# Retention and a Swish layer in one kernel: a fence for each half of the output banks, four up tiles in token halves, two groups of batch 1 a half-up sooner

## The chip, the cores and the metric

The kernel runs on one core of a Trainium2 chip. The core has five engines that run on their own and wait for one another by semaphores: TensorE (PE in the profile; its weight loads are PEld), VectorE (DVE), ScalarE (ACT), GpSimd (POOL) and SyncE (SP), which here issues the DMAs. TensorE multiplies a loaded operand of up to 128 x 128 by a moving one and writes to PSUM, eight banks of 128 partitions. The metric is the device time of one execution in microseconds (us). Before the change the median of 3 runs is 292.82 us (292.6 to 293.25).

## The reference

There are 8 batches, 8 heads, 576 positions and a head size of 64. A retention layer without softmax comes first: scores of q and k, weighted with a decay by distance and cut off above the diagonal, times v. Its output, 4608 tokens of 512 features, goes through two matrix products with a Swish between them.

```python
scores = scale * np.matmul(q, k.transpose(0, 1, 3, 2))
gamma = 1.0 - 2.0 ** (-5.0 - np.arange(H, dtype=np.float32))
Dmat = np.where(rel >= 0, gamma[:, None, None] ** rel[None, :, :], 0.0)
attn = np.matmul(scores * Dmat, v)                 # rel = position of the query less that of the key
x = attn.transpose(0, 2, 1, 3).reshape(B * S, H * D)
h = x @ w_in                                       # 512 -> 2048
out = (h / (1.0 + np.exp(-beta * h))) @ w_out      # 2048 -> 512
```

## The kernel before

**Blocks.** The first 512 positions of each batch are a block of 512 tokens (blocks 0 to 7). The last 64 positions of all eight batches form block 8, the "tails". For each block the retention output is made transposed in `xT` (features on the partitions, in four chunks `ko` of 128), and then come 16 "ups": `up(m, fo)` multiplies a 128-wide tile of `w_in` by the block's `xT`, four matmuls of 512 columns that add up in one PSUM bank, and ACT takes Swish of it into `gT` (L775; from block 3 on every other tile goes by way of `hs`, L772, and DVE, L773). `up(m, fo, c0, cn)` with `cn=2` is a half-up: the same tile for half of the block's tokens, four matmuls of 256 columns. Blocks 0 to 2 then multiply `gT` by `w_out` directly (`down`, L893). From block 3 on the second product is made by seven products of quarter size instead of eight: DVE adds pairs of quarters of `gT` into `sa` (L789), and PE multiplies in the chains U, W and Z (L805).

**Retention.** With the decay folded into q, k and v as gains by position, the work of a batch falls into small matmuls on quarters of TensorE's array: 64 rows by 64 columns each, named by `half(x)` or `row_d(j)`, the first or second 64 partitions. `paired` (L544) writes two lists alternately, so that neighbouring matmuls use different halves of the rows. For batches 2 to 7, `scores` makes the masked score tiles `R`, the states (running sums of k times v over chunks of positions, in `sbd` and `sbq`) are made by `one_state` and added up by `fold`, and `both4` makes the block's output in four PSUM banks `O4[x, y]`, x the parity of the chunk and y the half of the heads:

- `outputs4` (L643): 64 matmuls of `vn` by `R` open and fill the banks, first for y = 0, then for y = 1.
- `fence` (L555): ACT copies 128 x 2 numbers (L556) after the last matmul written so far. Nobody reads the copy; it is there so that the next matmul of another row half on the same bank can wait for it.
- `crosses4` (L661): 56 matmuls of the states by q add the part that comes from earlier chunks. They are 28 pairs, j = 0 and j = 1. j is the row half, and the column half is j for y = 0 and 1 - j for y = 1. Each j first adds to the banks x = j and then to the others. The first cross of j = 0 on x = 1 waits for the fence, the thirteenth pair where nothing else lies between. In batches 3, 5 and 6 sixteen pairs of the next batch's states (`ahead`) stand between the two parts. In both parts y is the innermost loop.

`tail_outputs` (L720) and `tail_crosses` (L735) do the same for the tails with 64 outputs and 64 crosses, and the fence is waited for behind the first 32. All of these matmuls are issued by `mm`, so the profile puts them on L550.

**Batch 1** is done in an older form, by groups (one group is one chunk of 128 positions; 4 to 7 are batch 1's). TensorE turns k around with `t_k` (L414, DVE copies the result, L415), `a_sc` makes scores that DVE masks (L448), `states` and `state_out` make the states, and `second(6)` makes the output of groups 6 and 7 and copies it to `xT` (L499).

**Order.** Engines take their instructions in the order in which the program writes them. `merged` (L913) writes a list of filling work, `fill` (ups, downs and the seven products), one entry after another, and before entry n all steps whose due time is at most n. `u1` is the place of block 1's first half-up. The ten half-ups from `u1` use the first half of block 1's tokens (groups 4 and 5), the ten after them the second half (groups 6 and 7). Their PSUM banks are three of the tag `mm`; scores of batch 1's last groups use the tags `sc` and `O`, two banks each, and `sc` is also where `t_k` puts its result.

Of the kernel before, what the change touches and what calls it, by code (L numbers as in the profile page):

```python
# [19 lines left out]
def kernel(  # L20
# [10 lines left out]
    nc = tc.nc  # L31
# [4 lines left out]
    P = 128  # L36
    HP = H // 2
    KO = d_model // P
    FO = d_ff // P
    MB = 512  # L40
    CB = MB // P
    PC = P // CB
    TL = S - MB
    NT = B // 2
# [5 lines left out]
    SB = 3  # L50
# [115 lines left out]
    for x in range(2):  # L166
        w = slice(x * TL, (x + 1) * TL)
# [15 lines left out]
    w_in_sb = wpool.tile([P, KO, d_ff], BF16, name="w_in_sb")  # L183
# [101 lines left out]
    xts = {}  # L285
# [6 lines left out]
    def F(f, *a):  # L292
        return lambda: f(*a)  # L293
# [4 lines left out]
    batch, pair, live = {}, {}, {}  # L298
# [118 lines left out]
    def q_cols(i, r, p, kind=None):  # L417

        b, c = seq[i]
        cols = slice(c * PC, (c + 1) * PC) if kind is None else slice(c * PC + kind * PC // 2, c * PC + (kind + 1) * PC // 2)  # L420
        return batch[b]["qT"][r, :, p, cols], lambda o: o.rearrange("k (i s) -> k i s", i=CB)
# [112 lines left out]
    def half(x):  # L534
        return slice(x * TL, (x + 1) * TL)

    def row_d(j):
        return slice(j * D, (j + 1) * D)

    def tile_of(c, kind):  # L540

        return c - c % 2 + (c % 2 if kind else 1 - c % 2)

    def paired(one, two):  # L544
        for a, b in zip(one, two, strict=True):
            a()
            b()

    def mm(out, lhsT, rhs, start=False, stop=True, after=None):
        ins = nc.tensor.matmul(out, lhsT, rhs, start=start, stop=stop, skip_group_check=True)  # L550
        if after:
            tc.add_manual_dep(ins.ins, after.pop().ins.name, ordered, reason="row tiles of one bank")
        last[0] = ins

    def fence():  # L555
        f = nc.scalar.copy(fenced[:], lscale[:].to_broadcast([P, 2]))  # L556
        tc.add_manual_dep(f.ins, last[0].ins.name, ordered, reason="row tiles of one bank")
        return [f]
# [13 lines left out]
    def state_banks():  # L572
        return [psum.tile([P, 2, HP, D], F32, name="st", tag=t, bufs=n) for t, n in (("mm", 3), ("st", 1))]
# [64 lines left out]
    def new_O4(lead, shape):  # L638
        live[lead]["O4"] = {(x, y): psum.tile(shape, F32, name="O", tag="sc" if x else "O", bufs=2)
                            for x in range(2) for y in range(2)}  # L640
        return live[lead]["O4"]

    def outputs4(b):  # L643

        i0 = b * CB
        O4, opened = new_O4(i0, [P, 2, CB, 2 * PC]), set()
        R = batch[b]["R"]

        def one(x, y, cc, pp, kind, hh):
            p, c = 2 * y + pp, 2 * cc + x  # L650
            w = cc * PC + kind * PC // 2
            mm(O4[x, y][row_d(hh), pp, :, w:w + PC // 2], live[i0 + tile_of(c, kind)]["vn"][half(x), 2 * p + hh, :],
               R[cc][half(x), hh ^ y, kind, p, :].rearrange("k (i s) -> k i s", i=CB), start=(x, y, hh) not in opened, stop=False)
            opened.add((x, y, hh))

        for y in range(2):
            paired(*[[F(one, x, y, cc, pp, kind, hh ^ x) for cc in range(2) for pp in range(2) for kind in range(2)
                      for hh in range(2)] for x in range(2)])
        batch[b]["O4"] = O4, fence()

    def crosses4(b, later=None):  # L661

        i0 = b * CB
        O4, after = batch[b]["O4"]

        def cross(j, e, y, pp, after):
            p, c, kind = 2 * y + pp, e // 2, e % 2
            w = c // 2 * PC + kind * PC // 2
            mm(O4[c % 2, y][row_d(j ^ y), pp, :, w:w + PC // 2], sbq[e - 1][row_d(j), p, :],
               q_cols(i0 + c, row_d(j), p, kind)[0], after=after)  # L670

        def crosses(j, x, after=None):
            return [F(cross, j, e, y, pp, after) for e in range(1, 2 * CB) if e // 2 % 2 == x for pp in range(2) for y in range(2)]

        ahead, bank = ([], []), None
        if b < B - 1 and b not in (XB, SB + 1):
            bank = state_banks()
            ahead = four_states(b + 1, 0, bank)
        paired(*[crosses(j, j) + ahead[j] + crosses(j, 1 - j, None if j else after) for j in range(2)])
        def out(n, x, y, O):  # L680
            to = xt(b)[:, 2 * y:2 * y + 2].rearrange("k p i (c x s) -> k (p i) c x s", c=2, x=2)[:, :, :, x, :]
            e = nc.scalar.copy if n == 1 or b > XB and n % 2 or later is not None else nc.vector.tensor_copy
            e(to, O[:].rearrange("k p i (c s) -> k (p i) c s", c=2))

        outs = [F(out, n, x, y, O) for n, ((x, y), O) in enumerate(O4.items())]
        if later is not None:
            casts = []
            if bank:
                fold(b + 1, 0, bank, casts=casts, by=nc.scalar.copy)
            later += outs + casts  # L690
            return
        for f in outs:
            f()
        if bank:
            fold(b + 1, 0, bank)
# [24 lines left out]
    def tail_outputs(i0):  # L720

        O4, opened, R = new_O4(i0, [P, 2, NT, TL]), set(), live[i0]["R"]

        def one(x, y, t, pp, hh):
            p = 2 * y + pp
            mm(O4[x, y][row_d(hh), pp, t, :], live[i0 + t]["vn"][half(x), 2 * p + hh, :],
               R[t // 2][half(x), hh ^ y, t % 2 * HP + p, :], start=(x, y, hh) not in opened, stop=False)
            opened.add((x, y, hh))

        for y in range(2):  # L730
            paired(*[[F(one, x, y, t, pp, hh ^ x) for t in range(NT) for pp in range(2) for hh in range(2)]
                     for x in range(2)])
        live[i0]["O4"] = O4, fence()

    def tail_crosses(i0, later):  # L735

        O4, after = live[i0]["O4"]

        def cross(j, x, t, y, pp, after):
            p = 2 * y + pp  # L740
            mm(O4[x, y][row_d(j ^ y), pp, t, :], ends[2 * t + x][row_d(j), p, :], live[i0 + t]["qkT"][row_d(j), 0, p, half(x)],
               after=after)

        for own in range(2):
            paired(*[[F(cross, j, j ^ own, t, y, pp, after if own else None) for t in range(NT) for pp in range(2) for y in range(2)]
                     for j in range(2)])
        def out(x, y, O):
            for r in range(2):
                to = xt(B)[:, 2 * y:2 * y + 2].rearrange("k p (a r) (s l x) -> k (p a) r l x s", r=2, l=2, x=2)[:, :, r, :, x, :]
                nc.scalar.copy(to, O[:].rearrange("k p (a l) (r s) -> k (p a) r l s", l=2, r=2)[:, :, r])  # L750

        later += [F(out, x, y, O) for (x, y), O in O4.items()]
# [4 lines left out]


    gts = {}

    def up(m, fo, c0=0, cn=CB):
        if m not in gts:
            gts[m] = sb.tile([P, FO, CB, P], BF16, name="gT", tag="gT", bufs=1)
        w = slice(c0 * PC, (c0 + cn) * PC)
        ph = psum.tile([P, CB, P], F32, name="ph", tag="mm", bufs=3)
        ph = ph.rearrange("f i s -> f (i s)")[:, :cn * P].rearrange("f (i s) -> f i s", i=CB)
        for ko in range(KO):
            nc.tensor.matmul(ph, w_in_sb[:, ko, fo * P:(fo + 1) * P], xts[m][:, ko, :, w],  # L768
                             start=(ko == 0), stop=(ko == KO - 1))
        if m >= SB and fo % 2:  # L770
            h = scratch[0][:, fo // 2 % 4].rearrange("f (i s) -> f i s", i=CB)
            nc.scalar.activation(h, ph, ACT.Silu, scale=beta_sb[:, fo:fo + 1])  # L772
            nc.vector.tensor_scalar(gts[m][:, fo], h, ratio[:, fo // 2:fo // 2 + 1], None, ALU.mult)  # L773
            return
        nc.scalar.activation(gts[m][:, fo, :, w], ph, ACT.Silu, scale=beta_sb[:, fo:fo + 1])  # L775
# [223 lines left out]
    d0 = len(fill)  # L999
# [9 lines left out]
    u1 = len(fill)  # L1009
# [12 lines left out]
    def second(i):  # L1022
# [3 lines left out]
        if i > CB:  # L1026
# [14 lines left out]
               [(d0 + 12.6, F(t_k, 1, 0, 0)), (d0 + 12.6, F(t_k, 1, 0, 1)), (d0 + 14, F(a_sc, 1, 0, 0)), (d0 + 14, F(a_sc, 1, 0, 1)),  # L1041
                (d0 + 14, F(states, 1, 0)), (d0 + 14, F(state_out, 1, 0)), (d0 + 14, F(state_out, 1, 1)), (d0 + 15.9, F(second, 4))],
               [(d0 + 10, F(pre_k, 1, 1, r)) for r in range(2)] + [(d0 + 12, F(pre_v, 1, 1, r)) for r in range(2)] +
               [(d0 + 15.95, F(t_k, 1, 1, 0)), (u1 + 1, F(t_k, 1, 1, 1)), (u1 + 3, F(a_sc, 1, 1, 0)), (u1 + 3, F(a_sc, 1, 1, 1)),
                (u1 + 3, F(states, 1, 2)), (u1 + 3, F(state_out, 1, 2)), (u1 + 8.5, F(second, 6))]]


    def group1(b, ccs):
# [31 lines left out]
    t = base[2]  # L1080
# [20 lines left out]
    for n in range(SB, B + 1):  # L1101
        t, m = base[n], blocks[n]
        first, second = slice(0, KH // 2), slice(KH // 2, KH)
# [10 lines left out]
    for n in range(1, B):  # L1114
# [3 lines left out]
        b, t = n + 1, base[n]  # L1118
# [61 lines left out]
```

## Time and profile before

| | |
|---|---|
| median of 3 runs | 292.82 us (292.6 to 293.25) |
| profiled execution, its own time | 293.46 us |
| its span in the profile | 291.8 us |
| granted TensorE clock | 1.000 |
| TensorE busy | 280.2 us, 96% |
| VectorE, ScalarE, GpSimd busy | 64%, 58%, 46% |

The profile is one execution, taken by the hardware. Its first part gives each engine's busy time; a list of waits gives who stood idle for whom; a timeline gives, for a stretch of time, the start of a row (us from the span's start), its length, engine, line, operation, output and inputs, shape and count, and in brackets the idle time before it with what ended it. `<-issue` means that nothing in the profile ended that idle time. Ends of matmuls are modelled: a row of n matmuls lasts from the first's start to the last's modelled end, so that neighbouring rows overlap by about 0.2 us. Where the text says "from start to start" it takes the starts alone.

### The profile page before, as it was taken

Reading aid. Unit: us, or ns where it says so; the run is one execution under the profiler, and the core shown is the slowest. Engines: PE = TensorE matmul, PEld = TensorE weight load, DVE = VectorE, ACT = ScalarE, POOL = GpSimd, SP = SyncE. Lnnn points to the kernel's source line nnn. Section 1 sums busy time; section 2 is a strip of 40 time slices with the busy share of each in tenths; the row PEclk is TensorE's granted clock in tenths of the full one; section 3 lists DMA queues with packets and bytes.
Section 4 is the critical chain, followed back from the end, with each engine's and each line's share of the span. In section 5 each row is a group of like instructions: output and inputs, shape, how many; then the busy total and the mean of one; then the engine's idle time right before and its main releaser. Section 6 shows DMA issues by size and latency. Waiting matters only on the chain.

```text
span 291.8 us, 8653 instructions
## 1 busy us (share of the span) xinstructions
PE 280.2 (96%) x3599; PEld 177.4 (61%) x3627; DVE 187.6 (64%) x347; ACT 169.5 (58%) x298; POOL 133.0 (46%) x258
## 2 busy tenths in 40 slices
PE   7899999999999999999999899999999999999995
PEld 5674446764544455548845685578557855784584
DVE  5974545704795296299598794986498545642673
ACT  4377636686968873674157514762476156837730
POOL 6366029924980972678583593434079300000000
PEclk9999999999999999999999999999999999999999
DMA  7999999969999999999999928960678530003004
GB/s 223 309 365 385 380 306 283 189 127 239 186 196 284 222 163 260 283 234 162 255 258 182 246 62 231 175 141 2 205 163 171 81 146 3 0 24 122 0 3 143
DMA packets 120568, 54.05 MB, mean 185 GB/s; under 512 B 93889, under 2 KB 113361, under 8 KB 120529
## 3 DMA queue, kind: packets, MB, share of 16 engines
q1 hardware_dynamic: 120496, 53.49, 76.5%
q8 instruction: 28, 0.46, 0.6%
q14 instruction: 12, 0.09, 0.1%
q10 hardware_dynamic: 32, 0.01, 0.0%
HBM read 36.71 MB, written 9.44 MB: 158 GB/s over the span
## 4 chain that ended last, share of the span: by engine, by line
PE 88%; DVE 5%; DMA 3%; issue 2%; SPq 1%; ACT 0%; POOL 0%; DVEq 0%
PE ph L768 37%; PE po L893 14%; PE U L805 10%; PE Z L805 7%; PE W L805 6%; PE O L550 4%; PE ph L860 4%; DMA kvn<-in_k_dram 3%; PE sc L550 2%; DVE sa L789 2%; PE st L550 2%; DVE sbd L293 1%; PE ph L875 1%; DVE sum L586 1%; PE st L510 1%
## 5 line engine op out<-in xcount | busy, mean ns | idle before, releaser
L768 PE MATMUL ph<-xT,w_in_sb 128*128 128x512 bf16 (+1 forms) x542 | 114.2, 363 | 2.2 <-issue 0.6
L768 PEld LDWEIGHTS <-w_in_sb 128*128 128x128 bf16 x560 | 53.5, 98 | 56.1 <-DVE sum L586 0.9
L775 ACT ACTIVATE gT<-ph,beta_sb 128x512 bf16<-128x512 f32 (+1 forms) x92 | 58.3, 640 | 44.5 <-PE ph L768 43.5
L805 PEld LDWEIGHTS <-sa 128*128 128x128 bf16 x480 | 46.9, 98 | 6.3 <-issue 0.6
L773 DVE TENSOR_SCALAR gT<-hs,ratio 128x512 bf16<-128x512 f32 x48 | 25.8, 539 | 34.4 <-ACT hs L772 33.9
L789 DVE TENSOR_TENSOR sa<-gT 128x1024 bf16<-128x1024 bf16 (+1 forms) x54 | 44.5, 866 | 0.7 <-PE Z L805 0.4
L330 POOL TENSOR_TENSOR qs<-qn,gq 128x256 bf16<-128x256 f32 x48 | 31.9, 696 | 28.1 <-DMA qn<-in_q_dram 20.8
L772 ACT ACTIVATE hs<-ph,beta_sb 128x512 f32<-128x512 f32 x48 | 33.0, 687 | 20.0 <-PE ph L768 19.7
L893 PE MATMUL po<-w_out_sb,gT 128*128 128x512 bf16 x184 | 42.0, 379 | 1.0 <-issue 0.8
L312 POOL TENSOR_TENSOR vn<-kvn,gv 128x256 bf16<-128x256 f32 x48 | 33.3, 714 | 7.6 <-issue 3.2
L367 POOL CAST kn<-kvn 128x128 bf16<-128x128 f32 (+1 forms) x72 | 25.0, 383 | 17.2 <-DMA kvn<-in_k_dram 17.1
L893 PEld LDWEIGHTS <-gT 128*128 128x128 bf16 x192 | 18.1, 98 | 20.9
L805 PE MATMUL U<-b,sa 128*128 128x256 bf16 x192 | 22.9, 273 | 0.4 <-DVE ot L819 0.4
L805 PE MATMUL Z<-b,sa 128*128 128x256 bf16 x192 | 23.1, 273 | 0.0
L293 DVE TENSOR_TENSOR R<-sc,late 128x512 bf16<-128x512 f32 x24 | 15.4, 679 | 11.2 <-issue 10.0
L805 PEld LDWEIGHTS <-gT 128*128 128x128 bf16 x192 | 18.7, 98 | 3.5
L255 DVE TENSOR_TENSOR b<-wt 128x512 bf16<-128x512 f32 x20 | 15.9, 851 | 1.9 <-ACT wt L238 1.8
L448 DVE TENSOR_TENSOR R<-sc,causal 128x512 bf16<-128x512 f32 x16 | 10.2, 682 | 2.2 <-PE sc L550 2.0
L379 POOL CAST kn<-kvn 128x512 bf16<-128x512 f32 x6 | 3.8, 653 | 16.9 <-DMA kvn<-in_k_dram 16.9
L805 PE MATMUL W<-b,gT 128*128 128x256 bf16 x96 | 11.5, 273 | 0.0
L805 PE MATMUL W<-b,sa 128*128 128x256 bf16 x96 | 11.5, 273 | 0.0
L805 PE MATMUL U<-b,gT 128*128 128x256 bf16 x96 | 11.5, 273 | 0.0
(121 smaller groups left out, 316.7 us busy)
## 6 DMA issues: line engine op xcount, KB each, us to landing
qn<-in_q_dram SPq DMA_DIRECT2D x16, 512.0 KB, 5.6
out_dram<-ot SPq DMA_DIRECT2D x32, 256.0 KB, 3.2
wt<-in_moe_w_out_dram SPq DMA_DIRECT2D x8, 512.0 KB, 9.4
kvn<-in_k_dram SPq DMA_DIRECT2D x12, 256.0 KB, 6.6
kvn<-in_v_dram SPq DMA_DIRECT2D x12, 256.0 KB, 5.9
kvn<-in_k_dram SPq DMA_DIRECT2D x24, 128.0 KB, 4.7
kvn<-in_v_dram SPq DMA_DIRECT2D x24, 128.0 KB, 3.8
wt<-in_moe_w_in_dram SPq DMA_DIRECT2D x5, 512.0 KB, 8.3
```

The source lines that it names most:

```text
L293: return lambda: f(*a)
L312: nc.gpsimd.tensor_tensor(vn[:, hs], v[:, hs], g[:, hs], ALU.mult)
L330: nc.gpsimd.tensor_tensor(batch[b]["qs"][:, cs, to], q_tiles[b][:, hs, cs].rearrange("p h i d -> p i h d"), gq[:, cs, hs].unsqueeze(3).to_ ...
L367: nc.gpsimd.tensor_copy(kn[:, c % 2, to], t[:, 0, hs])
L550: ins = nc.tensor.matmul(out, lhsT, rhs, start=start, stop=stop, skip_group_check=True)
L768: nc.tensor.matmul(ph, w_in_sb[:, ko, fo * P:(fo + 1) * P], xts[m][:, ko, :, w], start=(ko == 0), stop=(ko == KO - 1))
L772: nc.scalar.activation(h, ph, ACT.Silu, scale=beta_sb[:, fo:fo + 1])
L773: nc.vector.tensor_scalar(gts[m][:, fo], h, ratio[:, fo // 2:fo // 2 + 1], None, ALU.mult)
L775: nc.scalar.activation(gts[m][:, fo, :, w], ph, ACT.Silu, scale=beta_sb[:, fo:fo + 1])
L789: nc.vector.tensor_tensor(sums_a[0][:, held_in[j], ks], quarter(m, *x, ks), quarter(m, *y, ks), op)
L805: nc.tensor.matmul(chains[c, n][:, 0 if alone else p], a, sevens[k // 2][:, j - 1, k % 2, :], start=j in (3, 4, 1) and k == 0 and (alone o ...
L893: nc.tensor.matmul(po[:, :nn], gT[:, fo, ms, :], w_out_sb[:, fo, n0:n0 + nn], start=(fo == 0), stop=(fo == FO - 1))
```

## The change

It has three parts.

1. `outputs4` and `tail_outputs` make a fence behind the outputs of y = 0 and another behind those of y = 1, and hand on a list of two. In the crosses y becomes the outermost loop in place of the innermost, and the first cross of j = 0 onto the other banks waits for the fence of its own y.
2. In `up`, for block 3 (`SB`) and the tiles 12 to 15, each matmul of 512 columns becomes two of 256, one for each half of the tokens, with the same loaded operand.
3. In batch 1's steps for the last two groups, scores, states and state copies are due at `u1 + 2` instead of `u1 + 3`, and the output of groups 6 and 7 at `u1 + 7.5` instead of `u1 + 8.5`; as entries are whole numbers, each is written one half-up sooner.

```diff
@@ outputs4 (tail_outputs alike)
+        after = []
         for y in range(2):
             paired(*[[F(one, x, y, cc, pp, kind, hh ^ x) for cc in range(2) for pp in range(2) for kind in range(2)
                       for hh in range(2)] for x in range(2)])
-        batch[b]["O4"] = O4, fence()
+            after.append(fence())
+        batch[b]["O4"] = O4, after
@@ crosses4
-        def crosses(j, x, after=None):
-            return [F(cross, j, e, y, pp, after) for e in range(1, 2 * CB) if e // 2 % 2 == x for pp in range(2) for y in range(2)]
+        def crosses(j, x, after=(None, None)):
+            return [F(cross, j, e, y, pp, after[y]) for y in range(2) for e in range(1, 2 * CB) if e // 2 % 2 == x for pp in range(2)]
...
-        paired(*[crosses(j, j) + ahead[j] + crosses(j, 1 - j, None if j else after) for j in range(2)])
+        paired(*[crosses(j, j) + ahead[j] + crosses(j, 1 - j, (None, None) if j else after) for j in range(2)])
@@ tail_crosses
-            paired(*[[F(cross, j, j ^ own, t, y, pp, after if own else None) for t in range(NT) for pp in range(2) for y in range(2)]
-                     for j in range(2)])
+            paired(*[[F(cross, j, j ^ own, t, y, pp, after[y] if own and not j else None) for y in range(2) for t in range(NT)
+                      for pp in range(2)] for j in range(2)])
@@ up
+    halved = (12, 13, 14, 15)
...
+        ns = 2 if m == SB and fo in halved else 1
         for ko in range(KO):
-            nc.tensor.matmul(ph, w_in_sb[:, ko, fo * P:(fo + 1) * P], xts[m][:, ko, :, w],
-                             start=(ko == 0), stop=(ko == KO - 1))
+            for n in range(ns):
+                cs = slice(n * CB // ns, (n + 1) * CB // ns)
+                nc.tensor.matmul(ph[:, cs], w_in_sb[:, ko, fo * P:(fo + 1) * P], xts[m][:, ko, cs, w],
+                                 start=(ko == 0 and n == 0), stop=(ko == KO - 1), skip_group_check=ns > 1)
@@ batch 1's steps
-               [(d0 + 15.95, F(t_k, 1, 1, 0)), (u1 + 1, F(t_k, 1, 1, 1)), (u1 + 3, F(a_sc, 1, 1, 0)), (u1 + 3, F(a_sc, 1, 1, 1)),
-                (u1 + 3, F(states, 1, 2)), (u1 + 3, F(state_out, 1, 2)), (u1 + 8.5, F(second, 6))]]
+               [(d0 + 15.95, F(t_k, 1, 1, 0)), (u1 + 1, F(t_k, 1, 1, 1)), (u1 + 2, F(a_sc, 1, 1, 0)), (u1 + 2, F(a_sc, 1, 1, 1)),
+                (u1 + 2, F(states, 1, 2)), (u1 + 2, F(state_out, 1, 2)), (u1 + 7.5, F(second, 6))]]
```

More of the change, by code (lines that the diff above doesn't have):

```diff
@@ L728, in one @@
             opened.add((x, y, hh))
+        after = []
         for y in range(2):
@@ L732, in tail_outputs @@
                      for x in range(2)])
-        live[i0]["O4"] = O4, fence()
+            after.append(fence())
+        live[i0]["O4"] = O4, after
     def tail_crosses(i0, later):
```

## The prediction

> **What bounds the kernel now.** First the page's head and queue table, then TensorE's (PE's) own waits (us in total, times, longest): is PE the bound, and where does it stand still?
>
> ```profile
> span 291.8 us, 8653 instructions
> PE 280.2 (96%) x3599; PEld 177.4 (61%) x3627; DVE 187.6 (64%) x347; ACT 169.5 (58%) x298; POOL 133.0 (46%) x258
> q8 instruction: 28, 0.46, 0.6%
> ...
> PE O L550 <- issue: 0.9, 1, 0.9
> PE U L805 <- DVE ot L819: 0.4, 1, 0.4
> PE ph L768 <- DVE xT L499: 0.2, 1, 0.2
> PE O L550 <- ACT fenced L556: 0.2, 1, 0.2
> ```
>
> PE is busy 96% and no other engine over 64%: what PE loses or gains goes to the end unless another engine takes it back. Its waits are few, and three of these four lie where the diff works. Next the timeline, by row, at those places (start, length, engine; idle before in brackets).
>
> ```profile
> 50.81 0.39 PE L414 MATMUL T<-ident,kn 128*128 128x128 bf16 x4
> 51.03 1.04 PE L768 MATMUL ph<-xT,w_in_sb 128*128 128x256 bf16 x8
> 51.23 0.42 DVE L415 COPY kT<-T 128x512 bf16<-128x512 bf16 x1 [0.53 <-PE T L414]
> 52.00 0.64 PE L550 MATMUL sc<-qT,kT 64*64 64x128 bf16 x32
> 52.47 0.42 PE L550 MATMUL st<-vn,kn 64*64 64x64 bf16 x16
> 56.55 1.29 DVE L499 CAST xT<-O 128x512 bf16<-128x512 f32 x2 [0.84 <-PE O L477]
> 57.04 0.61 PE L768 MATMUL ph<-xT,w_in_sb 128*128 128x256 bf16 x4
> 57.90 0.50 PE L768 MATMUL ph<-xT,w_in_sb 128*128 128x256 bf16 x3 [0.25 <-DVE xT L499]
> ```
>
> That is batch 1: one half-up (four matmuls) covers DVE's copies of groups 6 and 7, and is too short.
>
> ```profile
> 79.46 0.71 PE L550 MATMUL O<-R,vn 64*64 64x64 bf16 x64
> 79.98 0.49 PE L550 MATMUL O<-qT,sbd 64*64 64x64 bf16 x24
> 80.41 0.19 ACT L556 COPY fenced<-lscale 128x2 f32<-128x2 f32 x1 [0.33 <-PE O L550]
> 80.66 0.21 PE L550 MATMUL O<-qT,sbd 64*64 64x64 bf16 x1 [0.18 <-ACT fenced L556]
> ...
> 161.82 0.25 PE L550 MATMUL O<-qT,sbd 64*64 64x64 bf16 x7 [0.94 <-issue]
> ```
>
> The first four are batch 2's fence: 64 outputs, 24 crosses, ACT's fence, then the other crosses. The last is batch 5, in its crosses: PE stands 0.94 us (1.12 from start to start) and nothing shown releases it.
>
> ```profile
> q8 instruction: 1, 0.02, 118.4%
> ```
>
> So the DMA view answers for 159.40 to 159.45: one packet of the instruction queue starts there; 118.4% of 16 engines over 0.05 us is 0.95 us. PE has 3627 loads and as many matmuls, 7254 instructions; 0.46 MB over that is 64 bytes each, so this queue is PE's, and a packet of 0.46 MB / 28 holds 256 instructions, 128 matmuls with their loads. The stall comes after 2137 loads, near instruction 4290. If that is a packet's edge, edges lie 256 apart. Against the packets' landings every other edge was reached 2.1 to 21 us after its packet had landed, without a stall; this one 0.28 us after, and PE went on 1.4 us after the landing. I read the stall as late instructions: batch 5's 64 outputs, 56 crosses and 32 states use 304 instructions in 1.4 us.
>
> **Batch 1 sooner.** Everything moves one half-up (0.435 us: four by 109 ns). After the move two half-ups lie between group 6/7's work and the first that needs their copies: the 0.41 us lost before 57.90 (57.04 + 0.435 against 57.90) goes. But only one lies between the last transposes and the scores, which need DVE's copy (51.23 to 51.65) and the bank it frees. Scores could start at 51.03 + 0.44 + 0.09 = 51.56; the copy lets them at 51.71. New wait 0.15. Behind the scores the six half-ups stay: DVE's four masks end 0.3 sooner, as does PE. The casts then end at 57.55, two half-ups at 57.62: no wait is left. Gain 0.41 - 0.15 = 0.26 to 0.28; I take **-0.28**. Ends: -0.41 (no wait for the copy) to 0. No DMA moves.
>
> **Four ups in halves.** 16 matmuls of 512 columns (216 ns apart) become 32 of 256 (109 ns): 16 x 2.6 ns = **+0.04**; the loads, 98 ns, still fit under 109. ACT and DVE see the same tiles. But 16 matmuls with their loads are 32 more PE instructions ahead of batch 5: its edge falls 32 earlier in the program, and what asks for the packet passes 16 ups (3.5 us) sooner, while the edge itself stays in the dense stretch. If a packet is asked for when PE's queue, some 40 instructions ahead of PE (the lead that fits the 28 landings best), enters the block before, this one was asked for at 156.9, 3.8 us before PE needed it; it would be 7.1 us, and landing plus 1.4 us took 4.9. So the stall goes. Batches 3 and 6, with the same order and no late packet, lose 0.10 to 0.13 at some point of the crosses, so I take **-1.0** of 1.12. Ends: 0 (it stays) and -1.12. What is late next: ACT's `hs` at 163.14 follows PE, DVE's seven sums follow it and hold PE's U at 170.71 (0.59 from start to start). That chain comes about 0.75 sooner; POOL's `qs` at 164.75 waits on a load and need not. Sums took 0.61 before POOL started and 0.81 to 1.06 beside it; one more outside is 0.2. I take **-0.1**, ends 0 and -0.3.
>
> The Trainium skill (Runtime: NRT & Kernel Launch, Instruction fetch mechanics) says that instructions are fetched in 16 KiB blocks of 256 and that crossing a block's edge is mostly hidden by the issue floor. The block size agrees with 0.46 MB / 28; by its second half these 32 instructions would buy nothing.
>
> **Fences and order.** Each output stage gets a second fence: ACT 0.19 us, seven times, waiting mid-outputs; nothing on ACT behind it can start before the old fence anyway. The last fence still follows the last output, so a wait on it shrinks only by what PE does before it: 16 crosses more.
>
> The price is in the new order. Rows of one group of four (both row halves by both column halves of the array) start 3 to 4 ns apart, and groups 31.6 ns apart: the outputs' x64 in 0.71 us, less one matmul's 0.21, is 8 ns each. The x16 `st` at 52.47 uses two quarters only: (0.42 - 0.19) / 15 = 15 ns, so a quarter takes a matmul each 31.6 ns. With y innermost, crosses of j = 0 and 1 go round all four quarters. With y outermost, each j stays on one quarter for six or eight in a row: two quarters at work, 31.6 ns a pair where it was 16 to 17. Of 28 pairs that is 0.42 us more PE time, unless it lies inside a fence's wait.
>
> Last cross, counted from the stage's first output (outputs take 0.50; fence to PE 0.25):
> - Batch 2: 0.51 + 12 pairs = 0.89; first fence 0.95; 8 pairs to 1.20, second at 1.20; ends 1.43, was 1.45: -0.02.
> - Batch 4: 0.89, 1.14, ends 1.36, was 1.35: +0.01.
> - Batch 7: ACT's Silu (217.58 + 0.69) holds the first fence until 218.25, the second 0.2 behind: PE at 1.03, ends 1.50, was 1.40: +0.10.
> - Tails: Silu until 246.71; first fence at 1.02, 16 pairs, ends 1.50, was 1.27: +0.23.
> - Batches 3, 5, 6: 32 state matmuls lie between, so the fence cost little. 32 of 44 pairs slow down; ends 1.63, was 1.50, 1.38 (stall left out) and 1.64: +0.14, +0.25, +0.01.
>
> Sum **+0.7**. Ends: the three long fence waits (0.35, 0.32, 0.29) and the tails' 0.22 all gone, -1.2; every pair's 15.6 ns exposed (6 x 28 + 32 = 200 pairs), +3.1. I stay by the `st` row, the nearest to what is added.
>
> **Sum.** -0.28 + 0.04 - 1.0 - 0.1 + 0.7 = -0.6 us. The profiled execution took 293.46 us (span 291.8 and 1.66 around it), 0.64 over the median 292.82. It would give 292.85, the median 292.2.
>
> **Rivals.**
> - *The order is free*: one quarter after another starts without the 31.6 ns. For it: the two rows of `st` share a row half, the new pairs do not. Against: each quarter repeats at 31.6 ns in every four-quarter row too. Then fences give -0.1 to -0.3: -1.5 in all, 291.3.
> - *The instruction wait stays or moves*. The added 32 shorten one other lead: the edge at 3522, reached at 137.95, was asked 5.6 us ahead and would be asked 4.6, in batch 4's W and Z; its packet took 2.75 from request to landing and 1.4 more, 4.15. From 0.5 us of DMA delay on, PE waits there; other packets took up to 3 us longer. With one such wait of 1.1, or the old one: 292.2 + 1.1 = 293.3, to 294.5 with the longest. This is the slower side. The skill's rule above would give this same case by calling the fetch hidden.
> - *Batch 1 gives nothing and the quarters cost more*: scores wait for the copy and the fence pairs drain: 0.28 + 0.4 dearer, 292.9.
>
> **How the numbers follow.** My forecast 45%, own range 291.8 to 292.7; order free 20%; wait stays or moves 20%; dearer 15%. 0.2% (0.59 us), about what a measurement can tell from no change, lies at 292.23 and 293.41. Faster: half of the first, all of the second and a little of the rest, 0.45. Slower: two thirds of the third, a third of the last, 0.18. Same 0.37. The range 291.3 to 293.5 leaves out half of the second and half of the third.
>
> **What would show it.** Right: no gap near 160.9 (less 0.3) and the packet before it landing over 2 us ahead; crosses in starts of two per 31.6 ns; no DVE wait before group 6's half-up, a 0.15 wait before batch 1's last scores; tails' crosses 0.2 us longer. Wrong: an "issue" gap of about 1 us anywhere, most likely at 135 to 138; crosses still four per 31.6 ns; PE waiting on DVE at 170 for as much more as the fetch saved.

## The result and the profile after

The changed kernel takes 292.15 us (median of 22 runs, 291.71 to 293.23), the kernel before 292.97 us beside it (22 runs, 291.89 to 295.19). The ratio is 0.9972 [0.9958, 0.9985], a gain of 0.82 us. Measured a second time the gain was smaller, 0.9993 [0.9978, 1.0009] (e11 below), so the honest size is some 0.2%, and the forecast of 292.2 us with -0.6 lies between the two. Two executions below ran at a granted clock of 0.977 (the profiled one of e4, 296.39 us, and one of the kernel before beside e12, 298.31 us): the ratios leave them out, and e4's profile is not read.

The profiled execution of the changed kernel took 292.35 us. Here are the lines of its page's head, of its queue table and of TensorE's waits that answer those of before.

```profile
span 290.6 us, 8728 instructions
PE 282.9 (97%) x3643; PEld 180.3 (62%) x3643; DVE 184.2 (63%) x347; ACT 170.5 (59%) x305; POOL 128.1 (44%) x258
q8 instruction: 28, 0.46, 0.7%
...
PE sc L550 <- ACT kT L415: 0.6, 2, 0.4
PE ph L776 <- DVE sum L586: 0.5, 1, 0.5
PE st L510 <- issue: 0.4, 1, 0.4
PE T L414 <- POOL kn L379: 0.2, 1, 0.2
PE ph L776 <- DVE xT L496: 0.2, 1, 0.2
```

All four waits of before that were shown are gone from the list: the 0.9 in the crosses, U for DVE's `ot`, the half-up for DVE's copy (L499) and the cross for its fence. (Some wait for the second fence is left, which the modelled ends of the matmuls cover: in batch 2 PE's loads pause for 0.18 us there, where it was 0.45.) Those for `sum`, `kn` and L496's `xT` were there before too, with 0.4, 0.5 and 0.2. New are 0.6 for ACT's `kT`, at 9.0 and 12.3 us, and 0.4 at L510; both lie at the start of the kernel, where the change does nothing, and the second comes back at the end of this document. (PE's busy time cannot be compared: before's trace lacks 28 matmul records, 3599 for 3627 loads, this one lacks none.) The timeline of after at the places that were shown of before: batch 1, batch 2's fences and batch 5.

```profile
51.07 0.39 PE L414 MATMUL T<-ident,kn 128*128 128x128 bf16 x4
51.30 0.60 PE L776 MATMUL ph<-xT,w_in_sb 128*128 128x256 bf16 x4
51.50 0.42 DVE L415 COPY kT<-T 128x512 bf16<-128x512 bf16 x1 [0.53 <-PE T L414]
51.83 0.79 PE L550 MATMUL sc<-qT,kT 64*64 64x128 bf16 x32
57.01 1.37 PE L776 MATMUL ph<-xT,w_in_sb 128*128 128x256 bf16 x11
...
79.44 0.71 PE L550 MATMUL O<-R,vn 64*64 64x64 bf16 x64
79.95 0.19 ACT L556 COPY fenced<-lscale 128x2 f32<-128x2 f32 x1
79.97 0.41 PE L550 MATMUL O<-qT,sbd 64*64 64x64 bf16 x16
80.37 0.19 ACT L556 COPY fenced<-lscale 128x2 f32<-128x2 f32 x1 [0.23 <-PE O L550]
80.46 0.54 PE L550 MATMUL O<-qT,sbd 64*64 64x64 bf16 x15
...
160.31 0.41 PE L550 MATMUL O<-qT,sbd 64*64 64x64 bf16 x16
```

In batch 1 the row of eleven matmuls of half-ups at 57.01 runs through without a wait, and the scores begin 0.53 us after the half-up, but their row is 0.79 long where it was 0.64: that is the wait for DVE's copy, 0.15 us, inside the row (two loads at 51.82, the third at 51.98, just behind the copy's end at 51.92). In batch 2 the crosses go (0.41 - 0.19) / 15 = 15 ns apiece, two per 31 ns, where four went in that time. In batch 5 no row has an "issue" behind it. The DMA view of after for 156.70 to 156.90 says where the packet went:

```profile
q8 instruction: 1, 0.02, 37.2%
```

37.2% of 16 engines over 0.2 us is 1.19 us; the packet starts at 156.80 and has landed at 158.00, 1.78 us before batch 5's first output (159.78). In the kernel before it landed 0.93 us after it.

**Where the time went**, by the differences of the same instructions' starts in the two profiles (after less before): start-up +0.25; batch 1 -0.28; the four halved ups +0.04 (from the first one's start to that of U's first matmul their 32 matmuls take 3.49 us, it was 3.45); output stages of batches 2 to 4 +0.1, and what lies between them +0.1; DVE's wait ahead of batch 5 +0.10; batch 5 -0.92; the stretch from 162 to 176, where U waited, -0.78; batch 6, 7 and the tails +0.03, +0.10 and +0.12.

### The profile page after: what moved, and what is told of

Same layout as the page of the kernel before. It is cut to its first block, busy times and chain, and to the rows that moved or that the text cites. A ratio compares the mean times of both kernels' runs of the same rounds, so it can differ in the third digit from the quotient of the medians.

```text
span 290.6 us, 8728 instructions
## 1 busy us (share of the span) xinstructions
PE 282.9 (97%) x3643; PEld 180.3 (62%) x3643; DVE 184.2 (63%) x347; ACT 170.5 (59%) x305; POOL 128.1 (44%) x258
## 4 chain that ended last, share of the span: by engine, by line
PE 94%; DVE 3%; DMA 1%; issue 1%; ACT 1%; DVEq 0%
PE ph L776 38%; PE po L901 15%; PE U L813 11%; PE W L813 7%; PE Z L813 7%; PE O L550 4%; PE ph L868 4%; PE sc L550 2%; PE st L550 2%; PE ph L269 1%; DMA beta_rows<-in_moe_beta_dram 1%; PE T L406 1%; PE T L414 1%; PE ph L883 1%; PE O L477 1%
## 5 line engine op out<-in xcount | busy, mean ns | idle before, releaser
L776 PE MATMUL ph<-xT,w_in_sb 128*128 128x512 bf16 (+1 forms) x576 | 116.5, 359 | 0.7 <-DVE sum L586 0.5
L776 PEld LDWEIGHTS <-w_in_sb 128*128 128x128 bf16 x576 | 55.1, 98 | 54.4 <-DVE sum L586 1.2
L330 POOL TENSOR_TENSOR qs<-qn,gq 128x256 bf16<-128x256 f32 x48 | 30.5, 667 | 30.4 <-DMA qn<-in_q_dram 21.6
L901 PE MATMUL po<-w_out_sb,gT 128*128 128x512 bf16 x192 | 43.3, 379 | 0.0
L797 DVE TENSOR_TENSOR sa<-gT 128x1024 bf16<-128x1024 bf16 (+1 forms) x54 | 42.1, 821 | 1.3 <-PE Z L813 1.2
L312 POOL TENSOR_TENSOR vn<-kvn,gv 128x256 bf16<-128x256 f32 x48 | 31.6, 681 | 8.0 <-issue 7.2
L367 POOL CAST kn<-kvn 128x128 bf16<-128x128 f32 (+1 forms) x72 | 24.4, 377 | 16.5 <-DMA kvn<-in_k_dram 16.5
L255 DVE TENSOR_TENSOR b<-wt 128x512 bf16<-128x512 f32 x20 | 14.8, 801 | 2.1 <-ACT wt L238 1.8
```

The source lines that it names most:

```text
L312: nc.gpsimd.tensor_tensor(vn[:, hs], v[:, hs], g[:, hs], ALU.mult)
L330: nc.gpsimd.tensor_tensor(batch[b]["qs"][:, cs, to], q_tiles[b][:, hs, cs].rearrange("p h i d -> p i h d"), gq[:, cs, hs].unsqueeze(3).to_ ...
L367: nc.gpsimd.tensor_copy(kn[:, c % 2, to], t[:, 0, hs])
L776: nc.tensor.matmul(ph[:, cs], w_in_sb[:, ko, fo * P:(fo + 1) * P], xts[m][:, ko, cs, w], start=(ko == 0 and n == 0), stop=(ko == KO - 1), ...
L797: nc.vector.tensor_tensor(sums_a[0][:, held_in[j], ks], quarter(m, *x, ks), quarter(m, *y, ks), op)
L901: nc.tensor.matmul(po[:, :nn], gT[:, fo, ms, :], w_out_sb[:, fo, n0:n0 + nn], start=(fo == 0), stop=(fo == FO - 1))
```

## The experiments

Each kernel is timed beside the kernel before; the brackets are 95% intervals. "Part 1" is fences and order, "part 2" the halves, "part 3" batch 1. The question is whether the halves act by the place of an instruction packet's edge, and whether part 1 costs what was worked out. The diffs are excerpts and show the lines that tell an edit: those of e2 and e4 against the changed kernel, those of e5, e6, e9 and e10 against e1, the others against the kernel before.

### One part alone, and the whole less one

**e1_halves**: part 2 alone.

```diff
+    halved = (12, 13, 14, 15)
+        ns = 2 if m == SB and fo in halved else 1
```

> The four tiles in halves alone, on the kernel before. Theory (late instructions): 32 more PE instructions ahead of batch 5 let its packet be asked for some 3.5 us sooner; the gap of about 1 us in batch 5's crosses is gone, its packet lands over 2 us ahead of use, and batch 5's stage (first output to the next up) falls from 2.6 to about 1.5 us. Time -1.0 us, and down to -1.8 if PE's wait for DVE near 170 goes with it. Rival (the fetch is hidden, the gap is something else): the gap stays, time +0.04 us.

291.99 against 292.82 us, 0.9966 [0.9947, 0.9985]. No "issue" row in batch 5's crosses; the stage takes 1.59 us (from its first output's load to the next up's). One of the three parts makes as much as the whole change did.

**e2_no_halves**: parts 1 and 3, without part 2.

```diff
-    halved = (12, 13, 14, 15)
-        ns = 2 if m == SB and fo in halved else 1
...
-            for n in range(ns):
...
+            nc.tensor.matmul(ph, w_in_sb[:, ko, fo * P:(fo + 1) * P], xts[m][:, ko, :, w],
+                             start=(ko == 0), stop=(ko == KO - 1))
```

> The whole change without the halves: two fences, y outermost, batch 1 sooner. Theory: the gap in batch 5's crosses is still there, somewhat shorter (0.8 to 1.1 us) since the slower order reaches the packet's edge later; fences and order +0.35 us (batch 5's share is hidden in the gap), batch 1 -0.27: within 0.2 us of before. Rival (the new order or the fences took the gap away): no gap, about -0.8 us.

293.36 against 292.82 us, 1.0009 [0.9992, 1.0027]: the gain is gone. Its profiled run had only 0.20 us of the stall left, since the packet happened to land at 159.42, 0.45 us earlier in the stage than before: the size of the stall varies from profile to profile.

**e3_order_and_fences**: part 1 alone.

```diff
-            return [F(cross, j, e, y, pp, after) for e in range(1, 2 * CB) if e // 2 % 2 == x for pp in range(2) for y in range(2)]
+            return [F(cross, j, e, y, pp, after[y]) for y in range(2) for e in range(1, 2 * CB) if e // 2 % 2 == x for pp in range(2)]
```

> Two fences and y outermost alone. Theory: crosses at two per 31.6 ns; the tails' stage 0.12 to 0.23 us longer, batches 3 and 7 about 0.1 longer, batches 2 and 4 unchanged, the gap in batch 5 stays: +0.3 to +0.5 us. Rival (the order is free and the fence waits go): -0.3 to -1.0 us.

293.68 against 292.82 us, 1.0027 [1.0009, 1.0046]: part 1 costs, 0.86 us by the medians; the +0.3 to +0.5 expected lie inside the interval. The stall is there, in its timeline:

```profile
163.51 0.35 PE L550 MATMUL O<-qT,sbd 64*64 64x64 bf16 x12 [1.09 <-issue]
```

**e4_halves_and_sooner** and, later, beside the whole change, **e12_halves_and_sooner_again**: parts 2 and 3, without part 1.

```diff
-            after.append(fence())
-        batch[b]["O4"] = O4, after
+        batch[b]["O4"] = O4, fence()
```

> Halves and batch 1 sooner, with the old single fence and the old order. Theory: the sum of what gains, -1.0 to -1.8 for the halves and -0.27 for batch 1: -1.3 to -2.1 us against before, 0.4 to 0.6 us faster than the whole change. Rival (the fences carry part of the gain): slower than the whole change.

> Halves and batch 1 sooner with the old fence and order, once more: stages 1.47, 1.6, 1.47, 1.6, 1.65, 1.45 and 1.39 us, no wait for DVE before group 6's half-up, no gap in batch 5; -1.1 to -1.4 us against before and 0.3 to 0.6 us faster than the whole change.

e4: 291.73 against 292.82 us, 0.9953 [0.9935, 0.9971]. e12: 291.71 against 293.08 us, 0.9956 [0.994, 0.9972]. Both times the change without its first part beats the kernel before by 0.45%.

**e11_whole_again**: the whole change once more, beside e12.

> The whole change once more, on this chip, beside the next kernel: -0.8 us against before; stages 1.5, 1.7, 1.55, 1.7, 1.8, 1.6 and 1.5 us for batches 2 to 7 and the tails.

292.69 against 293.08 us, 0.9993 [0.9978, 1.0009], half of what was expected. Between e11 and e12, whose intervals do not overlap, lies part 1: 0.98 us by the medians.

### What the halves do

If their 32 instructions only move the packets' edges, then the same 32 behind batch 5 do nothing, the same 32 anywhere ahead do all, and fewer do less.

**e6_halves_later**: the same four tiles, but of block 5, whose ups come after the stall.

```diff
-        ns = 2 if m == SB and fo in halved else 1
+        ns = 2 if m == SB + 2 and fo in halved else 1
```

> The same four tiles in halves, but in block 5, behind batch 5's crosses instead of ahead of them. Theory: nothing moves before batch 5; the gap of 0.4 to 1.3 us is there as before, time within 0.2% of before (+0.04 us). Rival (halved tiles help where they stand, by the bank, the clock or the waits): about -0.8 us, no gap.

293.12 against 292.91 us, 1.0009 [0.9986, 1.0031]. Its timeline has the stall whole:

```profile
161.86 0.25 PE L550 MATMUL O<-qT,sbd 64*64 64x64 bf16 x7 [1.08 <-issue]
```

**e10_halves_block2**: the same four tiles of block 2, which PE does some 60 us ahead of the stall.

```diff
-        ns = 2 if m == SB and fo in halved else 1
+        ns = 2 if m == 2 and fo in halved else 1
```

> The four tiles in halves in block 2 in place of block 3: the same 32 instructions, earlier still. Theory (only the count ahead of batch 5 matters): landing 1.0 to 1.8 us ahead of batch 5's stage, no gap there, and no new one in batches 3 and 4; -0.8 us, as with block 3's tiles. Rival (it has to be block 3's last tiles, just ahead of the seven products): the gap stays, no gain.

291.95 against 293.08 us, 0.9958 [0.994, 0.9976]. No gap in batch 5, its stage 1.50 us, the packet landed 1.19 us ahead of it. So it is not block 3's tiles, nor who waits for them: what e1 and e10 have in common, and e6 lacks, is 32 more instructions ahead of the stall.

**e5_one_tile** and **e9_two_tiles**: one tile of block 3 (8 instructions) and two (16). The excerpt is e5's; e9 has `(14, 15)`.

```diff
-    halved = (12, 13, 14, 15)
+    halved = (15,)
```

> Only tile 15 of block 3 in halves, on the kernel before: 8 more PE instructions ahead of batch 5 in place of 32. Theory: the packet is asked for four ups (0.87 us) sooner, so of the 0.9 to 1.3 us gaps seen, 0 to 0.4 us is left; the gap ends 1.3 to 1.5 us after the packet's landing as in the other kernels. Time -0.6 to -0.9 us. Rival (any shift of the block edge does it, or the split as such): the gap is gone wholly, or wholly there.

> Tiles 14 and 15 of block 3 in halves, on the kernel before: 16 more PE instructions ahead of batch 5. One tile (8) moved neither the packet's landing (1.0 us into batch 5's stage, 0.9 before) nor the gap; four (32) moved the landing to 1.4 to 1.8 us ahead of the stage. If the landing follows the request alone, 16 would bring it to about 0.8 us ahead and the gap away, -0.8 us; if it is set by the DMA traffic in which the packet waits, it stays near 1.0 us into the stage and the gap of 0.8 to 1.1 us stays, time as with one tile (-0.3 us), or it falls in between.

e5: 292.64 against 292.91 us, 0.999 [0.9974, 1.0006], unclear, with 0.84 us of stall left, where at most 0.4 was expected. e9: 291.89 against 293.08 us, 0.9974 [0.995, 0.9998], with 0.23 us left. The timeline of e5, then that of e9:

```profile
161.75 0.28 PE L550 MATMUL O<-qT,sbd 64*64 64x64 bf16 x11 [0.84 <-issue]
```

```profile
160.52 0.31 PE L550 MATMUL O<-qT,sbd 64*64 64x64 bf16 x15 [0.23 <-issue]
```

These two and the others give a row of sizes. The landing is that of the packet, counted from the stage's first output. The next column is the start of PE's 2137th load, the last one ahead of the stall (in the last row the load of the same count), counted from the landing; PE's resumption is counted from the landing too. Each list goes in the order of its kernels.

| instructions added ahead | kernels | packet lands, us | 2137th load after, us | PE idle, us | PE resumes after, us |
|---|---|---|---|---|---|
| 0 | before, e2, e3, e6, e7, e8 | +0.93, +0.48, +1.32, +1.03, +1.18, +0.95 | 0.28, 0.93, 0.11, 0.20, 0.09, 0.36 | 0.94, 0.20, 1.09, 1.08, 1.18, 0.78 | 1.32 to 1.50 |
| 8 | e5 | +1.00 | 0.32 | 0.84 | 1.39 |
| 16 | e9 | +0.20 | 1.03 | 0.23 | 1.46 |
| 32 | after, e1, e10, e11, e12 | -1.78, -1.36, -1.19, -1.67, -1.49 | 2.98, 2.51, 2.29, 3.03, 2.69 | none | |

Broadly, the sooner after the landing PE has used up its 2137 loads, the longer it stands: 1.18 us where it gets there 0.09 us after the landing, 0.20 where it gets there 0.93 after, nothing at 2.3 or more.

The windows view, from the start up to a moment inside the gap, counts what has gone by; its PEld column is the number of loads. For the kernel before, for e3, whose crosses stand in the new order, and for e9, two of whose tiles are in halves:

```profile
0.00:160.75 160.75, 155.22 (x2120) 91.05 (x2137) 103.56 (x207) 102.08 (x184) 94.91 (x198) 1.00 1.03 249
```

```profile
0.00:162.90 162.90, 155.80 (x2120) 91.06 (x2137) 105.69 (x209) 102.93 (x188) 97.18 (x198) 1.00 1.02 244
```

```profile
0.00:160.40 160.40, 154.82 (x2120) 91.56 (x2137) 103.26 (x207) 102.10 (x184) 95.86 (x198) 1.00 1.01 247
```

The place in the program differs, the count does not: PE stops after 2137 loads in each (and in e2, e5, e6, e7 and e8 too). That, the packet landing each time 1.3 to 1.5 us before PE goes on, and e6 against e10, show the stall to be one for instructions at a fixed count.

### What the fences and the order cost

**e7_two_fences_old_order**: the second fence, with y innermost as before.

```diff
-            return [F(cross, j, e, y, pp, after) for e in range(1, 2 * CB) if e // 2 % 2 == x for pp in range(2) for y in range(2)]
+            return [F(cross, j, e, y, pp, after[y]) for e in range(1, 2 * CB) if e // 2 % 2 == x for pp in range(2) for y in range(2)]
```

> Two fences, each with its own waiter, but y innermost as before. Theory (the order is what costs): four crosses per 31.6 ns again, stages as before within 0.05 us in batches 2 to 6; batch 7 and the tails up to 0.2 us longer, since ACT makes the second fence 0.2 us after the first; +0.1 to +0.4 us. Rival (the extra ACT fence costs): every stage some 0.1 us longer, as in the whole change.

293.0 against 292.91 us, 1.0005 [0.9983, 1.0026]: no difference that the interval could tell.

**e8_one_fence_new_order**: one fence as before, y outermost.

```diff
-            return [F(cross, j, e, y, pp, after) for e in range(1, 2 * CB) if e // 2 % 2 == x for pp in range(2) for y in range(2)]
+            return [F(cross, j, e, y, pp, after) for y in range(2) for e in range(1, 2 * CB) if e // 2 % 2 == x for pp in range(2)]
```

> One fence, y outermost. Theory: two crosses per 31.6 ns and the whole fence wait: stages of batches 2, 4, 7 and the tails about 0.25 us longer than before (1.7 to 1.8, 1.7, 1.65 to 1.75 and 1.65), batches 3, 5 and 6 as in the whole change; about +1.3 to +1.6 us with the gap in batch 5 still there. Rival (the second fence buys nothing): the same stages as the whole change.

293.51 against 292.91 us, 1.0024 [1.0003, 1.0045]: dearer, but by 0.60 us and not by the 1.3 to 1.6 expected. The stages, from their first output's load to the next stage's first load, in us (means over the kernels with that order and fences, and differences of the unrounded means; batch 5 only where there is no stall):

| stage | old order, one fence (7 kernels) | new order, two fences (4) | difference | predicted | two fences alone, e7 | new order alone, e8 |
|---|---|---|---|---|---|---|
| batch 2 | 1.53 | 1.56 | +0.04 | -0.02 | 1.64 | 1.69 |
| batch 3 | 1.63 | 1.70 | +0.07 | +0.14 | 1.67 | 1.62 |
| batch 4 | 1.55 | 1.60 | +0.05 | +0.01 | 1.55 | 1.69 |
| batch 5 | 1.62 | 1.79 | +0.17 | +0.25 | | |
| batch 6 | 1.71 | 1.76 | +0.05 | +0.01 | 1.67 | 1.73 |
| batch 7 | 1.46 | 1.59 | +0.13 | +0.10 | 1.61 | 1.57 |
| tails | 1.39 | 1.52 | +0.13 | +0.23 | 1.52 | 1.54 |
| sum | | | +0.64 | +0.72 | | |

The same stage also differs among kernels with the same order and fences, most in batch 3 (1.50 in e5 and e9, 1.86 in e10), and e7 and e8 are one profile each. So the rows of batches 2 to 6 are not clear of that spread one by one; the tails' is (1.39 to 1.40 in the seven, 1.52 in the four).

In batches 2 and 4 the order alone costs 0.16 and 0.14 (its 1.69 lies above all seven of the old order there), and with the second fence only 0.04 and 0.05. As I read it, there the fence of y = 0 comes early enough to win back most of it. In batch 7 and in the tails the second fence alone costs 0.15 and 0.13, the order alone 0.11 and 0.15, and both together no more than either: there the fences lie on ACT behind a Silu, the second 0.2 to 0.3 us behind the first, and, as far as these rows tell, the slower pairs pass while PE would wait.

## Why the prediction was right, step by step

**The step on late instructions was right and carries the result.** Without the stall the time falls by 0.34% (e1) to 0.42% (e10), 0.83 to 1.13 us with the halves' own price in it, where -1.0 and +0.04 were taken. The mean batch 5 stage without a stall, 1.62 us in the old order and 1.79 in the new with both fences, is 0.9 to 1.3 us shorter than the stages with a stall of 0.78 or more. Its rival, that the wait stays or moves, falls: no PE wait appears in batch 4's W and Z in any of the kernels with 32 instructions. The Trainium skill (Runtime: NRT & Kernel Launch, Instruction fetch mechanics) has blocks of 256 instructions, which agrees with 28 packets of 0.46 MB in all. It calls the crossing of an edge mostly hidden, which holds for most edges here; at one edge it does not, at 0.20 to 1.18 us in the eight profiles with fewer than 32 instructions added ahead.

**How much sooner the packet comes was over-estimated.** It was to land 3.5 us sooner for the 32 instructions; the means of the table, counted from the stage's first output, are +0.98 and -1.50, 2.5 us. It was also to land over 2 us ahead of its use, and that came true: PE gets to the end of its 2137 loads 2.3 to 3.0 us after the landing, where the working gives 3.6 (the 7.1 us from request to need, less the 3.5 that the landing took). Eight instructions did nothing that shows among landings that vary by 0.8 us without any change. So the lead of some 40 instructions is not shown, and what delays this one packet stays open; no run here varied the DMA traffic alone. The margin sufficed in all five profiles.

**Batch 1 was exact.** From its first half-up to block 1's first `down` it took 16.88 us before and in all kernels without part 3, and 16.60 in after, e2, e11 and e12: -0.28, of 0.41 gained and 0.15 given back in the wait for the copy.

**The halves cost what was worked out**, +0.04 us: from the start of the four tiles' first matmul to that of U's first it takes 3.45 us with 512 columns (before, e2, e6, e10) and 3.49 with 256 (after, e1, e11, e12). With one tile in halves (e5) it is 3.46, with two (e9) 3.47.

**Fences and order: +0.64 measured by stages, +0.7 predicted.** The medians give +0.86 (e3) and +0.98 (e12 to e11), each uncertain by about 0.5. The cause is the one that was worked out, a quarter of the array that takes a matmul only each 31.6 ns, and the rival that the order is free falls. So does the one in which batch 1 gives nothing; the quarters were not dearer by its 0.4 in the stages, though the medians leave room for it. The pieces are less exact than the sum: the tails +0.13 for +0.23, batch 6 +0.05 for +0.01; that the sum comes so close is in part luck. e7 shows a part that was too small in the working: the second fence itself costs 0.13 to 0.15 where ACT is late.

**PE's wait for U was taken for lasting, and is not.** It went altogether, -0.78 us for the forecast -0.1, and nothing here ties that to the change. e10 has no stall in batch 5 and still has the wait; e12 has neither. The timeline of e10, then of e12:

```profile
163.39 5.79 DVE L793 TENSOR_TENSOR sa<-gT 128x1024 bf16<-128x1024 bf16 x6
163.88 7.91 POOL L330 TENSOR_TENSOR qs<-qn,gq 128x256 bf16<-128x256 f32 x8 [2.27 <-issue]
169.84 1.36 PE L809 MATMUL U<-b,sa 128*128 128x256 bf16 x11 [0.43 <-DVE ot L823]
```

```profile
163.11 3.69 DVE L793 TENSOR_TENSOR sa<-gT 128x1024 bf16<-128x1024 bf16 x6
168.07 3.14 POOL L330 TENSOR_TENSOR qs<-qn,gq 128x256 bf16<-128x256 f32 x4 [5.93 <-DMA qn<-in_q_dram]
```

The same six sums take 5.79 us beside POOL's `qs` and 3.69 without. In e12 POOL starts late, for it waits on a load of q. In the profiles of before, e6, e7 and e10 POOL starts at most 0.5 us behind the sums and PE waits; in the others it starts 2.6 us or more behind them and PE does not. (The Trainium skill, SBUF, Who interferes with whom, has a VectorE instruction with two SBUF inputs contend with a GpSimd instruction that reads SBUF; the two rows agree.) e2, e3 and e8 lack the wait and do not have part 2, and e1 lacks it without parts 1 and 3, so no one part is needed to take it away; what goes with it in all thirteen profiles read is when POOL starts. So 0.78 of the 1.11 us between the two profiles are most likely not the change's; no experiment moved the load alone.

**The sum.** -0.28 (batch 1), +0.64 (part 1) and -0.83 to -1.13 (part 2 with its price) make -0.5 to -0.8 us, or 0.997 to 0.998, around the forecast -0.6 and between the two measurements of the whole. The profiles' own difference of 1.11 us is no test of it: the U wait stands in it on the one side and start-up's +0.25 on the other, and neither is shown to be the change's.

## What to carry to other kernels

A gap on the bounding engine that no semaphore ends, with a packet of the instruction queue landing shortly before it ends, can be a wait for instructions. To tell, count what the engine has done when it stops, and add a few dozen instructions ahead of it or behind it: here 32 ahead took the gap away from two places, and 32 behind left it. Do not credit the edit's stated content with such a gain. Where small matmuls sit on quarters of the array, count how many quarters are at work in turn before reordering for a shorter wait: the faster kernel here is the one without the new order (e12, 0.9956). And compare two single profiles only after asking, of each difference, whether a third kernel without the edit shows it too.

## What the runs showed that was not expected

A second wait of the same kind stands at start-up in after, e2, e3, e5, e6, e10 and e11, and in no kernel is the program changed there. The timeline of e11:

```profile
20.35 0.34 PE L510 MATMUL st<-vn,kn 64*128 64x128 bf16 x3 [0.40 <-issue]
```

PE stops after 223 loads, 0.3 to 0.6 us, and goes on 1.2 to 1.6 us after the first instruction packet landed (17.3 to 19.0 us). It was not in the profile of before, and the prediction has no term for it. But the edge was there to be seen: in before PE's 224th load starts 1.74 us after the first packet's landing (18.88 and 17.14), less than the 2.1 us that the prediction counts as the least of the other edges. Whether the +0.25 at start-up comes of this wait stays open: e1, which does not show it, is at its first half-up at 50.91, after at 50.62. The two stops lie 2137 - 223 = 1914 loads apart, with as many matmuls 3828 instructions, within twelve of 15 times 256 (3840), and PE has a few others besides. So both fit one grid of 256, as the packets' size says, and at the other edges the waits of after name no "issue".
